# A gated mix of attention and a GEGLU layer: the order of head chains, last rows and one eviction around a nested product

## The chip, the cores and the metric

The kernel runs on one core of one Trainium2 chip. Its time is the device time of one execution in microseconds. The median of three runs of the kernel before is 1605.64 us (1605.62 to 1605.66). Engines are named as in the profile: PE is the matrix engine, DVE the vector engine, ACT the scalar engine, POOL the engine also called GpSimd, SP the one that issues the DMAs.

## The reference

Two branches over the same x (2048 tokens of 576 numbers) are mixed by a gate for each token:

```python
g = sigmoid((x * gate_w).sum(-1, keepdims=True))
a = attention(x, wq, wk, wv, wo, beta)        # 32 heads of 18, four segments of 512 tokens with a memory
b = (gelu(x @ w_gate) * (x @ w_up)) @ w_down  # 4608 hidden columns
return g * a + (1 - g) * b
```

For this change it matters that the second branch is three large products over 4608 hidden columns, and that the softmax of 128 pieces (a head, a segment) is worked in between them.

## The kernel before

**Steps.** The hidden columns are cut into 36 groups of 128, f, and the tokens into two halves, p. Each pair (f, p) is one call of `step(v)` (line 1428 on), v = 2f + p, 72 in all. Four steps make a block, fb = v // 4, and i4 = v % 4 is the place in it. A step computes gate and up of 128 hidden columns for 1024 tokens, by a scheme of Strassen's kind: sums of blocks of the weights are multiplied with sums of blocks of x, in three PSUM banks named V, G (in the code X) and U (in the code Y), and copies and adds on DVE carry one result into the next. Every operand is a pair of f16 parts, high and low, so each product is three matmuls for each block of rows: high by high, high by low, low by high. `product` (line 527) issues six matmuls of 512 columns, `rest` (1299) and `low_rests` (1304) the last 64 rows of the 576.

**The nested product.** In blocks from fb = 1 on, the product in V of the block's first group (i4 = 0 and 1) is itself split by the same scheme into seven products of 256 columns. Six of them are computed ahead, in the step before the one that needs them, in four pieces, `nest(at, 0)` to `nest(at, 3)` (line 1380): steps with i4 = 3 compute them for the next block's i4 = 0, steps with i4 = 0 for i4 = 1. I call these two the carrying steps, and the steps that use the result (i4 = 0 and 1) the nested steps. Piece 2, which the text calls the third, is six matmuls, the last three into the half A of bank V, which DVE then adds to a held tile (line 1401). Piece 3, the fourth, is three matmuls into A again, and so waits for that add; DVE adds it too (1404). The seventh, `nest_last` (1406), stands in the nested step, behind X's first product.

**The down chains.** The third product, with w_down, runs one block late: `chains` (1266) calls `down` (1248) for 32 chains of a block, eight in each step. A chain is six matmuls of 288 columns into a bank dn (of two), and one DVE instruction (1264) that adds it to the result. `early` are the step's first five, `late` the last three. It reads w_down's pairs (`paird`, low part by POOL, line 402) and the hidden values' pairs (`hh`, tiles hhr and hhd, high part by ACT, 1286, low part by POOL, 1294).

**The softmax.** `scores(a)` (1160) issues four matmuls: two into st banks, one of 256 columns into dn, one of 128 into pv or, for odd a, the other dn. DVE masks each and takes its maximum (1174). `powers` (1179) makes the exponentials on ACT and their pairs on POOL, and issues two transposing DMAs on SP. `values` (1197) is 20 short matmuls from them into bank pv, `normalize` (1212) what DVE does with the result.

**The end of a step.** `hidden` (1276) evicts bank G or U on DVE, times the gelu, into the hidden values; `end_pair` (1415), at the start of the next step, does this for the step before, and in between takes the mask passes of the last scores, first the dn pieces. In carrying steps `end_first` (1411) evicts G within the step itself. `hidden_pair` (1283) makes the pairs; in steps with i4 = 3 it leaves one low part on a list, which `hidden_lows` (1291) empties.

**What sets the order.** All four compute engines run in the order written in the code, so a step's text is the order of four queues; between engines only data and buffers make one wait for another. Where a step's call is moved, all that it issues on PE and DVE moves with it.

Of the kernel before, what the change touches and what calls it, by code (L numbers as in the profile page):

```python
# [43 lines left out]
def kernel(ctx: ExitStack, tc: tile.TileContext, xs, wqk, wv, wo, wgu, wd, beta, out):  # L44
# [8 lines left out]
    def bank(tag, bufs=1, dt=F32):  # L53
        return ps.tile([P, 512 if dt == F32 else 1024], dt, name=tag, tag=tag, bufs=bufs)
# [249 lines left out]
    def scale_g(f, cols=slice(0, KT * P)):  # L304
        if f < NF:
            r = raw_g[f].rearrange("p (a b) -> p a b", a=2)[:, :, cols]
            dve.tensor_scalar(r, r, scl[f // 2][0][:, 0:1], None, OP.mult)
# [16 lines left out]
    def sums_g(f):  # L324
        if f >= NF:
            return
        r = raw_g[f]
        g0, g2, u0, u2 = (r[:, o : o + 2 * P] for o in (0, 2 * P, KW, KW + 2 * P))
        g4, u4 = r[:, 4 * P : KW], r[:, KW + 4 * P :]
        pool.tensor_tensor(g2, g0, g2, OP.add)  # L330
        if f < 2 or f % 2 == 0:
            pool.tensor_tensor(g0, u0, g0, OP.subtract)
        pool.tensor_tensor(u0, g2, u0, OP.subtract)
        pool.tensor_tensor(u2, u2, u0, OP.subtract)
        pool.tensor_tensor(g4, u4, g4, OP.subtract)
# [7 lines left out]
    def low_g(f, b):  # L343
        for p in parts_g(f, b):
            pool.tensor_tensor(spot(f, *p, 1), raw_g[f][:, p[0] : p[1]], spot(f, *p, 0), OP.subtract)  # L345
# [18 lines left out]
    def nest_odd(b):  # L364
        if b < NB:
            nest_w[b] = nest_tile()
            r = raw_g[2 * b + 1]
            pool.tensor_tensor(nest_part(b)[1], r[:, KW : KW + 2 * P], r[:, : 2 * P], OP.subtract)

    def nest_pairs(b, i, what):  # L370
        if b >= NB:
            return
        a, r = nest_part(b)
        src, o = ((a, W00), (r[:, P:], W11), (r, WS3), (a, WS2))[i]
        n = src.shape[1]
        hi, lo = (nest_w[b][:, (o + 7 * j) * P : (o + 7 * j) * P + n] for j in range(2))
        if "h" in what:
            act.activation(hi, src, AF.Copy)
        if "l" in what:
            pool.tensor_tensor(lo, src, hi, OP.subtract)  # L380
# [11 lines left out]
    def scale_d(f):  # L392
        r = raw_d[f]
        dve.tensor_scalar(r, r, scl[f // 2 + 1][0][:, 1:2], None, OP.mult)
# [5 lines left out]
    def low_d(f):  # L400
        t = pair_d[f]
        pool.tensor_tensor(t[:, 1], raw_d.pop(f), t[:, 0], OP.subtract)  # L402
# [702 lines left out]
    with tc.tile_pool(name="keep", bufs=2, side="right", reuse_waits="tile") as kp, ExitStack() as tail:  # L1105
# [91 lines left out]
        def values(a):  # L1197
            kk, e = divmod(a, 2)
            if e == 0:
                pvb[kk] = bank("pv")  # L1200
            o = pvb[kk]
            pr = turned_p.pop(a)
            v = vts[kk // 4]
            c0 = (kk % 4) * VC
            for qi in range(4):
                ov = o[:, (4 * e + qi) * VC : (4 * e + qi + 1) * VC]
                for kb in range(qi + 1):
                    for i in range(2):
                        pe.matmul(ov, pr[:, 10 * i + COL[qi] // P + kb], v[:, 4 * e + kb, c0 : c0 + VC],  # L1209
                                  start=kb == 0 and i == 0, stop=kb == qi and i == 1)  # L1210
# [80 lines left out]
        def hidden_lows():  # L1291
            while lows:
                hh, t = lows.pop()
                pool.tensor_tensor(hh[:, 1], t, hh[:, 0], OP.subtract)
# [23 lines left out]
        def weights_nest(fb, i4, at):  # L1318
            if i4 == 1 and at == 2 and fb:
                for f in (2 * fb, 2 * fb + 1):  # L1320
                    scale_d(f)
            if i4 == 2 and at == 1:
                if fb:
                    scale_g(2 * fb + 3, FRONT)
                    sums_g(2 * fb + 2)
                nest_odd(fb + 1)
            if i4 == 2 and at == "late":
                for i in range(2):
                    nest_pairs(fb + 1, i, "hl")
                nest_sums(fb + 1)  # L1330
            if i4 == 2 and at == 2:
                for i in (2,) if fb else (2, 3):
                    nest_pairs(fb + 1, i, "hl")
            if i4 == 3 and at == 0 and fb:
                nest_pairs(fb + 1, 3, "hl")
                hidden_lows()

        def weights_high(fb, i4):
            n0 = 2 * fb
# [4 lines left out]
        def weights_low(fb, i4):  # L1344
            n0 = 2 * fb
            low_g(n0 + 1 + i4 // 2, i4 % 2)
            if i4 == 3:
                for f in (n0, n0 + 1):
                    low_d(f)

        def weights_load(fb, i4):
            n0 = 2 * fb
            if i4 == 1:
                load_g(n0 + 4)
            if i4 == 0 and fb:
                load_d(n0)
                load_d(n0 + 1)
            if i4 == 3:
                load_g(n0 + 5)
# [20 lines left out]
        def nest(at, n):  # L1380

            if at is None:
                return
            b, p = at
            if n == 0:
                nested[at] = bank("V")
                holds[p] = kp.tile([P, L], F32, name=f"hold{p}", bufs=1)
            B, A = (nested[at][:, i * HX : (i + 1) * HX] for i in range(2))
            h0, h1 = (holds[p][:, i * HX : (i + 1) * HX] for i in range(2))
            if n == 0:  # L1390
                nest_product(b, B, W00, X00, p, True)
                nest_product(b, A, WS3, XT3, p)
                dve.tensor_copy(h1, A)
            if n == 1:
                nest_product(b, A, W11, XT4, p)
                dve.tensor_copy(h0, A)
                dve.tensor_copy(A, B)
            if n == 2:
                nest_product(b, B, W01, X10, p)
                nest_product(b, A, WS2, XT2, p)  # L1400
                dve.tensor_tensor(h0, A, h0, OP.add)  # L1401
            if n == 3:
                nest_product(b, A, WS1, XT1, p)
                dve.tensor_tensor(h1, A, h1, OP.add)
# [6 lines left out]
        def end_first():  # L1411
            hidden(*ends[0])
            ends[0] = ends[0] + (True,)
# [14 lines left out]
        def step(v):  # L1428

            f, p = divmod(v, 2)  # L1430
            fb, i4 = divmod(v, 4)
            c, e = 2 * p, 2 * p + 1
            k = v - LAG
            on = lambda i: 0 <= i < 2 * H
            early = range(8 * i4, 8 * i4 + 5)
            late = range(8 * i4 + 5, 8 * i4 + 8)
            some = lambda b, js: chains(b, js) if b >= 0 else None
# [13 lines left out]
            at = (fb + 1, 0) if i4 == 3 and fb + 1 < NB else (fb, 1) if i4 == 0 and fb else None  # L1451
            if not fb:
                V, g1 = ahead.pop(v) if v in ahead else first_product(v)
            elif i4 < 2:
                V, g1 = nested[fb, p], gl_tile()
                if v != 4:
                    some(fb - 1, early[:1])
            else:
                V, g1 = bank("V"), holds[p]
                product(V, f, A22, x2_, 0, 4, True)  # L1460
            X, Y = bank("G"), bank("U")
            product(X, f, A11, x1, 0, 4, True)
            one = (2 if fb and i4 < 2 else 1) + (v == 4)
            if v == 4:
                dve.tensor_copy(Y, X)
                nest((1, 0), 2)
                some(0, early[:2])
                nest((1, 0), 3)
                some(0, early[2:3])
                nest_last(fb, V, p)  # L1470
                dve.tensor_copy(g1, V)
                nest_pairs_x(1, 1)
                some(0, early[3:4])
            elif fb and i4 < 2:
                nest_last(fb, V, p)
                dve.tensor_copy(g1, V)
                dve.tensor_copy(Y, X)
                put(2 * k - 1, 3)
                if on(k - 2):
                    values(2 * k - 3)  # L1480
            else:
                put(2 * k - 1, 3)
                dve.tensor_copy(Y, X)
# [6 lines left out]
            if v == 1:  # L1490
                scale_result()
            if v != 4:
                some(fb - 1, early[1 if fb and i4 < 2 else 0 : one])
            put(2 * k - 1, 2)
            puts.pop(2 * k - 1, None)
            if on(k - 2) and not (fb and i4 < 2):
# [13 lines left out]
            if fb:  # L1510
                weights_high(fb, i4)
                weights_low(fb, i4)
            weights_load(fb, i4)
            if v == 2 * NF - 2:
                sums_a(0)
# [77 lines left out]
            some(fb - 1, late[1:])  # L1593
            if on(k - 1):
                values(2 * k - 2)
            if v != 3:
                nest(at, 2)
            if low is not None:
                result_low(low)
            if fb:  # L1600
                low_rests(f, (X, U4, x1), (Y, UG, x2_))
                ends.append((f, c, X, g0))
                if at:
                    end_first()
            if on(k):
                puts[2 * k + 1] = scores(2 * k + 1)
            if v != 3:
# [159 lines left out]
        with tc.manual_schedule(engines=ORDERED):  # L1767
# [17 lines left out]
            fb = NB - 1  # L1785
# [88 lines left out]
```

## Time and profile before

| | |
|---|---|
| median of three runs | 1605.64 us |
| profiled execution | 1604.89 us |
| its span | 1603.2 us |
| granted PE clock | 1.000 |
| PE, DVE, ACT, POOL busy | 1559.9, 1257.4, 1208.8, 1123.7 us |

The span goes from the first to the last instruction of the profiled execution. Lines of a timeline begin with the start and the length in us from the span's start; a line can stand for several equal instructions in a row (x6), and its length then goes from the first one's start to the last one's end. A matmul's end is modelled: 512 columns are shown with 0.38 us, but six in a row start 0.215 us apart. In brackets stands for how long the engine was idle before, and what released it.

### The profile page before, as it was taken

To read this page: it belongs to the slowest core of one execution; us is meant where nothing else is said; L and a number is where in the kernel's file an instruction comes from. 1 tells how busy PE (TensorE), PEld (TensorE's weight loads), DVE (VectorE), ACT (ScalarE), POOL (GpSimd) and SP (SyncE) were. 2 spreads that over 40 slices of the span, in tenths; PEclk is the share of its full clock that TensorE was granted. 3 is DMA by queue.
4 is the path that set the end of the run, shared out by engine and by line. 5 is a ranking of instruction groups with operands and counts; after the bars stand their busy time and mean duration, and the time that the engine had idled before them with its cause. 6 is when DMAs were issued, how large, how long until landed. Compare 5 with 4: busy or idle time off the path is not lost.

```text
span 1603.2 us, 33958 instructions
## 1 busy us (share of the span) xinstructions
PE 1559.9 (97%) x12220; PEld 955.2 (60%) x12220; DVE 1257.4 (78%) x3254; ACT 1208.8 (75%) x2059; POOL 1123.7 (70%) x1220
## 2 busy tenths in 40 slices
PE   9999999999999999999999999999999999999999
PEld 5665655555555555556555555565555556556577
DVE  6788976778787888778787878787888778787565
ACT  7567544888888888888888888888888888787421
POOL 4345555877786868686776777776868686777597
PEclk9999999999999999999999999999999999999999
DMA  6534332576868687676777686879687777764546
GB/s 231 211 127 135 118 116 60 114 133 120 148 118 147 129 125 140 121 132 130 127 123 132 119 145 121 146 120 152 131 128 130 134 134 132 131 111 96 119 85 168
DMA packets 472833, 209.97 MB, mean 131 GB/s; under 512 B 427688, under 2 KB 437416, under 8 KB 472152
## 3 DMA queue, kind: packets, MB, share of 16 engines
q1 hardware_dynamic: 472664, 207.80, 65.7%
q8 instruction: 96, 1.57, 0.4%
q14 instruction: 73, 0.60, 0.1%
HBM read 91.87 MB, written 27.26 MB: 74 GB/s over the span
## 4 chain that ended last, share of the span: by engine, by line
PE 62%; POOL 12%; DVE 3%; ACT 3%; issue 1%; POOLq 0%; ACTq 0%; DVEq 0%
PE dn L1256 20%; PE U L532 14%; PE G L532 9%; PE V L532 5%; PE pv L1209 3%; PE V L1377 3%; POOL paird L402 2%; POOL pairg L345 2%; POOL pb L1192 2%; PE U L1302 1%; PE V L1307 1%; DVE gl L1279 1%; POOL x L1707 1%; PE V L1302 1%; POOL pairg L1690 1%
## 5 line engine op out<-in xcount | busy, mean ns | idle before, releaser
L1192 POOL TENSOR_TENSOR pb<-pb,ph 128x896 f16<-128x896 f32 (+1 forms) x256 | 368.4, 1439 | 273.2 <-ACT ph L1191 263.2
L532 PEld LDWEIGHTS <-pairg 128*128 128x128 f16 x2592 | 250.6, 98 | 261.4 <-issue 12.4
L1256 PE MATMUL dn<-paird,hhr 128*128 128x288 f16 x2115 | 331.3, 286 | 24.3 <-DVE mx L1174 20.9
L1190 ACT ACTIVATE pb<-pb,mb,esc 128x512 f32<-128x512 f32 (+3 forms) x512 | 305.0, 643 | 5.5 <-issue 0.4
L1264 DVE SCALAR_TENSOR_TENSOR acc<-dn,ev,acc 128x288 f32<-128x288 f32 x533 | 265.2, 513 | 45.8 <-PE dn L1256 38.5
L1256 PEld LDWEIGHTS <-hhr 128*128 128x128 f16 x2160 | 205.5, 98 | 106.7 <-issue 41.5
L1256 PE MATMUL dn<-paird,hhd 128*128 128x288 f16 x1275 | 211.7, 286 | 10.7 <-DVE mx L1174 7.0
L532 PE MATMUL G<-x,pairg 128*128 128x512 f16 x864 | 209.9, 379 | 1.1 <-DVE gl L1279 1.0
L532 PE MATMUL U<-xt,pairg 128*128 128x512 f16 x864 | 209.9, 379 | 0.0
L1191 ACT ACTIVATE ph<-pb 128x896 f16<-128x896 f32 (+1 forms) x256 | 188.5, 736 | 8.1
L345 POOL TENSOR_TENSOR pairg<-raw,pairg 128x384 f16<-128x384 f32 (+2 forms) x144 | 157.8, 1117 | 17.7 <-ACT pairg L341 17.7
L1256 PEld LDWEIGHTS <-hhd 128*128 128x128 f16 x1296 | 123.7, 98 | 63.6 <-issue 20.5
L1174 DVE CUSTOM_DVE_ANT_0 pb<-st,mask 128x512 f32<-128x512 f32 (+1 forms) x256 | 157.0, 613 | 0.0
L1174 DVE CUSTOM_DVE_ANT_0 pb<-dn,mask 128x256 f32<-128x256 f32 (+1 forms) x192 | 67.0, 374 | 91.7 <-PE dn L1171 89.9
L1185 ACT ACTIVATE mb<-mx,esc 128x4 f32<-128x4 f32 x128 | 36.8, 288 | 103.3 <-DVE mx L1174 103.3
L1377 PE MATMUL V<-xt,nest 128*128 128x256 f16 x714 | 105.9, 272 | 0.3 <-DVE hold L1401 0.2
L532 PE MATMUL U<-x,pairg 128*128 128x512 f16 x432 | 105.0, 379 | 0.4 <-DVE gl L1554 0.3
L532 PE MATMUL V<-x,pairg 128*128 128x512 f16 x426 | 103.9, 380 | 0.2
L1297 ACT ACTIVATE gl<-gl,sc 128x512 f32<-128x512 f32 x110 | 75.7, 714 | 29.8 <-DVE gl L1554 18.2
L1209 PEld LDWEIGHTS <-pt 128*128 128x128 f16 x2560 | 83.4, 96 | 5.5
L1209 PE MATMUL pv<-vt,pt 128*128 128x37 f16 x2560 | 84.6, 179 | 0.0
L1297 ACT ACT_TABLE_LOAD x65 | 83.4, 1283 | 1.1
(369 smaller groups left out, 3100.5 us busy)
## 6 DMA issues: line engine op xcount, KB each, us to landing
raw<-in_wgu_dram SPq DMA_DIRECT2D x36, 640.0 KB
rawd<-in_wd_dram SPq DMA_DIRECT2D x36, 288.0 KB
qt<-qk SPq DMA_DIRECT2D x132, 72.0 KB
kt<-qk SPq DMA_DIRECT2D x132, 72.0 KB
qk<-stage SPq DMA_DIRECT2D x36, 256.0 KB
qt<-qk SPq DMA_DIRECT2D x132, 36.0 KB
kt<-qk SPq DMA_DIRECT2D x132, 36.0 KB
vp<-vstage SPq DMA_DIRECT2D x16, 296.0 KB
```

The lines of the kernel that those rows point to most:

```text
L345: pool.tensor_tensor(spot(f, *p, 1), raw_g[f][:, p[0] : p[1]], spot(f, *p, 0), OP.subtract)
L532: pe.matmul(o, w[:, i, (a + k) * P : (a + k + 1) * P], x[:, b + k], start=start and k == 0 and i == 0 and b == h, stop=k == 1 and i == 1, ...
L1174: dve.tensor_tensor_reduce(scored(a, qi), out[qi], mask[:, L - (qi + 1) * P :], 1.0, -3e38, OP.add, OP.max, mx[a][:, qi : qi + 1])
L1185: act.activation(b, mx.pop(a), AF.Copy, bias=LN256, scale=esc[:, 1, c : c + 1])
L1190: act.activation(r, r, AF.Exp, bias=b[:, qi : qi + 1], scale=esc[:, 0, c : c + 1])
L1191: act.activation(h[:, cols], p, AF.Copy)
L1192: pool.tensor_tensor(low[:, cols], p, h[:, cols], OP.subtract)
L1209: pe.matmul(ov, pr[:, 10 * i + COL[qi] // P + kb], v[:, 4 * e + kb, c0 : c0 + VC], start=kb == 0 and i == 0, stop=kb == qi and i == 1)
L1256: pe.matmul(o[:, :NH], hh[:, a, q * P : (q + 1) * P], w[:, b, n * NH : (n + 1) * NH], start=i == 0, stop=i == 5)
L1264: dve.scalar_tensor_tensor(av, o[:, :NH], ev, av, OP.mult, OP.add)
L1297: act.activation(t, o, AF.Gelu_apprx_tanh, scale=scl[f // 2][0][:, 2 + c : 3 + c])
L1377: pe.matmul(o, w[:, (7 * c + i) * P : (7 * c + i + 1) * P], x[d], start=start and n == 0, stop=n == 2, skip_group_check=True)
```

## The change

Four moves, none of which adds or drops an instruction of the computation:

- In nested steps (but v = 4) the first down chain goes from ahead of X's product to behind the last nested product and the copies of V and X, next to the second one.
- In the same steps the values of the score before last go from ahead of the second chain to behind it.
- In steps with i4 = 3, the low part of hh that was left on the list is made behind the low parts of the next weights on POOL, not ahead of them.
- In carrying steps (but v = 3) the last rows of G and U and G's eviction go ahead of the third nested piece.

```diff
@@ weights_nest
             if i4 == 3 and at == 0 and fb:
                 nest_pairs(fb + 1, 3, "hl")
-                hidden_lows()
@@ step
             elif i4 < 2:
                 V, g1 = nested[fb, p], gl_tile()
-                if v != 4:
-                    some(fb - 1, early[:1])
@@ step
                 dve.tensor_copy(g1, V)
                 dve.tensor_copy(Y, X)
                 put(2 * k - 1, 3)
-                if on(k - 2):
-                    values(2 * k - 3)
             else:
                 put(2 * k - 1, 3)
                 dve.tensor_copy(Y, X)
@@ step
             if v != 4:
-                some(fb - 1, early[1 if fb and i4 < 2 else 0 : one])
+                some(fb - 1, early[:one])
+                if fb and i4 < 2 and on(k - 2):
+                    values(2 * k - 3)
             put(2 * k - 1, 2)
@@ step
             if fb:
                 weights_high(fb, i4)
                 weights_low(fb, i4)
+                hidden_lows()
             weights_load(fb, i4)
@@ step
                 values(2 * k - 2)
-            if v != 3:
-                nest(at, 2)
             if low is not None:
                 result_low(low)
             if fb:
@@ step
                 ends.append((f, c, X, g0))
                 if at:
                     end_first()
+            if v != 3:
+                nest(at, 2)
             if on(k):
                 puts[2 * k + 1] = scores(2 * k + 1)
```

## The prediction

> **What bounds the kernel.** I read the busy line of the page first, then the waits of PE, then the timeline of one block, engine by engine.
>
> ```profile
> PE 1559.9 (97%) x12220; PEld 955.2 (60%) x12220; DVE 1257.4 (78%) x3254; ACT 1208.8 (75%) x2059; POOL 1123.7 (70%) x1220
> ```
>
> PE is busy for 1559.9 of 1603.2 us, so a change of order can win about what PE idles, 43 us by this count. PE's rows in the view of waits say where most of it lies (us in total, times, longest):
>
> ```profile
> PE dn L1256 <- DVE mx L1174: 27.8, 32, 0.9
> PE dn L1256 <- POOL paird L402: 6.9, 14, 0.5
> ...
> PE V L1377 <- DVE hold L1401: 0.2, 1, 0.2
> ```
>
> Two kinds of wait make 34.7 us, both at a down chain (line 1256), and both so even (27.8/32 = 0.87, 6.9/14 = 0.49) that one block can stand for all. Both lie at the first head chain of a nested step. Here is PE from the end of a step with i4 = 0 into the one with i4 = 1:
>
> ```profile
> 724.54 0.81 PE L1377 MATMUL V<-xt,nest 128*128 128x256 f16 x6
> 725.28 0.39 PE L1307 MATMUL G<-x,pairg 64*128 64x512 f16 x1
> ...
> 725.51 0.38 PE L1171 MATMUL st<-kt,qt 54*128 54x512 f16 x2
> ...
> 725.88 0.50 PE L1377 MATMUL V<-xt,nest 128*128 128x256 f16 x3
> 727.25 0.53 PE L1256 MATMUL dn<-paird,hhr 128*128 128x288 f16 x3 [0.87 <-DVE mx L1174]
> ...
> 727.98 1.46 PE L532 MATMUL G<-x,pairg 128*128 128x512 f16 x6
> 729.28 0.49 PE L1377 MATMUL V<-xt,nest 128*128 128x256 f16 x3
> 729.61 0.67 PE L1209 MATMUL pv<-vt,pt 128*128 128x37 f16 x20
> 730.12 0.53 PE L1256 MATMUL dn<-paird,hhr 128*128 128x288 f16 x3
> ```
>
> In order: the third nested piece, the last rows, the scores, the fourth piece, the first head chain after its wait, X's product, the last nested product, the values, the second head chain. From start to start X's product takes 1.30 us and the last nested product 0.33; the fourth piece, of the same shape, is thus issued by 725.88 + 0.33 = 726.21, and PE issues nothing until 727.25: 1.04 us (the view says 0.87, since it counts from the modelled end of the matmul before). What the chain waits for is on DVE:
>
> ```profile
> 724.12 0.93 DVE L1264 SCALAR_TENSOR_TENSOR acc<-dn,ev,acc 128x288 f32<-128x288 f32 x2
> 725.39 0.42 DVE L1401 TENSOR_TENSOR hold<-V,hold 128x256 f32<-128x256 f32 x1 [0.34 <-PE V L1377]
> 725.78 0.75 DVE L1279 SCALAR_TENSOR_TENSOR gl<-G,sc,gl 128x512 f32<-128x512 f32 x1
> 726.45 0.41 DVE L1404 TENSOR_TENSOR hold<-V,hold 128x256 f32<-128x256 f32 x1
> 726.78 0.41 DVE L1174 CUSTOM_DVE_ANT_0 pb<-dn,mask 128x256 f32<-128x256 f32 x1
> ...
> 727.12 0.28 DVE L1174 CUSTOM_DVE_ANT_0 pb<-dn,mask 128x128 f32<-128x128 f32 x1
> ```
>
> The scores hold both dn banks; DVE frees the first at about 727.2, after the add of the third piece, G's eviction and the add of the fourth. X's product writes G and needs only that eviction, over at 726.53. The step with i4 = 0 begins in the same way, with POOL as a second wait (rows of POOL, DVE, ACT and PE in order of time):
>
> ```profile
> 701.80 1.16 POOL L1294 TENSOR_TENSOR hhd<-gl,hhd 128x512 f16<-128x512 f32 x1
> ...
> 702.92 2.04 POOL L345 TENSOR_TENSOR pairg<-raw,pairg 128x384 f16<-128x384 f32 x2
> ...
> 703.22 0.93 DVE L1264 SCALAR_TENSOR_TENSOR acc<-dn,ev,acc 128x288 f32<-128x288 f32 x2
> ...
> 703.44 0.71 ACT L1297 ACTIVATE gl<-gl,sc 128x512 f32<-128x512 f32 x1
> ...
> 704.48 0.42 DVE L1401 TENSOR_TENSOR hold<-V,hold 128x256 f32<-128x256 f32 x1 [0.33 <-PE V L1377]
> ...
> 704.91 2.51 POOL L402 TENSOR_TENSOR paird<-rawd,paird 128x576 f16<-128x576 f32 x2
> ...
> 704.97 0.50 PE L1377 MATMUL V<-xt,nest 128*128 128x256 f16 x3
> ...
> 706.34 0.53 PE L1256 MATMUL dn<-paird,hhr 128*128 128x288 f16 x3 [0.87 <-DVE mx L1174]
> 706.71 0.28 PE L1256 MATMUL dn<-paird,hhd 128*128 128x288 f16 x1
> ...
> 707.48 0.41 PE L1256 MATMUL dn<-paird,hhd 128*128 128x288 f16 x2 [0.48 <-POOL paird L402]
> ...
> 707.72 1.46 PE L532 MATMUL G<-x,pairg 128*128 128x512 f16 x6
> ...
> 710.58 1.46 PE L532 MATMUL V<-x,pairg 128*128 128x512 f16 x6
> ```
>
> **The head chains move behind the nested product.** No matmul is added or dropped, so only idle time changes. X's product and the last nested product, 1.30 + 0.33 = 1.63 us, now stand between the fourth piece and the first chain. That is more than the 1.04 us for which the chain waited, so this idle time goes: 32 x 1.04 = 33.3 us. At i4 = 0 the chain's fifth matmul was due at 706.34 + 4 x 0.12 = 706.83 (three take 0.37) and came at 707.48: 0.65 us, 14 times, 9.1 us. POOL is done by 704.91 + 2.51 = 707.42. In the new order the fourth piece starts at 705.36 (below), X's product at 705.69, the chain at 707.32, its fifth matmul at 707.8. The wait goes, by 0.4 us. Together 42.4 us.
>
> **What is late next.** X's product wants G; the last nested product wants the add of the fourth piece, 1.30 us back; V's product wants V copied, and there the two chains and the values (0.73 + 0.73 + 0.51 us, by the starts above) stand as cover instead of one chain and the values. On DVE the first chain's eviction falls behind the two copies and the 512 wide mask pass; the next user of a dn bank comes behind V's and Y's products, so nobody waits. The values come later in the step, yet hardly later on the clock: at i4 = 1 at 726.56 (below) + 1.63 + 2 x 0.73 = 729.65 against 729.61, at i4 = 0 sooner; their readers on DVE stand behind the eviction of Y. Cost of these: nothing. If the cover went, each would cost what it is short, at most 0.5 us in 16 steps, 8 us.
>
> **The held low part on POOL.** In steps with i4 = 3, hh's low part (1.16 us) goes behind two pairg and two paird subtractions. POOL's sum is the same, and the order of these alone changes; paird is ready 1.1 us sooner, and hh's low part last, at 707.42. The first chain of the next step reads it in its sixth matmul, at about 707.9: 0.5 us of room. Elsewhere the list is empty and the moved call does nothing. ACT's queue is not touched; the result's low part, with its DMAs, falls in steps with i4 = 2, in which no piece is moved, so SP's queue is not crossed either.
>
> **Last rows and G's eviction ahead of the third piece.** PE does the same work in another order. On DVE the eviction (0.67 us from start to start: 725.78 to 726.45) now stands ahead of the add that the fourth piece waits for. The last rows start where the third piece did, 724.54, plus a gap of 0.1 (such as lies between the third piece's six matmuls, 6 x 0.11, and 725.28), and G is complete 0.39 later, at 725.03; DVE is free at 725.05. So the eviction starts at 725.07, the add at 725.74, not 725.39: 0.35 later. The fourth piece came 725.88 - 725.39 = 0.49 after the add's start, though the scores in between were short enough; it does so again, 0.35 later. This is a new idle gap. At i4 = 3 the eviction needs also the gelu that ACT ends at 703.44 + 0.71 = 704.15, as DVE gets free (703.22 + 0.93); eviction 704.20, add 704.87, fourth piece 705.36 instead of 704.97: 0.39. Sum: 16 x 0.35 + 16 x 0.39 = 11.8 us, plus about 0.6 us in the last step of this kind, where no scores stand in between (the eviction's 0.67 less the gap of 0.1; its fourth piece waits already):
>
> ```profile
> 1477.41 0.49 PE L1377 MATMUL V<-xt,nest 128*128 128x256 f16 x3 [0.19 <-DVE hold L1401]
> ```
>
> It pays for itself only in that X's product finds G free. Without it, X's product would start after the eviction, at 726.53 + 0.06; with it, at 725.88 + 0.35 + 0.33 = 726.56. This part alone is therefore worth nothing, by these rows, and the bounds of the gap are 0 (the add is not held up) and 0.75 us (the eviction comes a whole length later).
>
> **The sum.** 42.4 - 11.8 - 0.6 = 30.0 us. From the profiled execution's 1604.89 us this makes 1574.9; the three timed runs lie 0.75 higher at their median, 1605.64, so the forecast is 1575.6 us.
>
> **A rule that bears on it.** The change brings DVE's scaling of the next weights forward against POOL:
>
> ```profile
> 712.13 1.15 POOL L1294 TENSOR_TENSOR hhr<-hold,hhr 128x512 f16<-128x512 f32 x1
> ...
> 712.26 1.44 DVE L307 TENSOR_SCALAR raw<-raw,sc 128x768 f32<-128x768 f32 x1
> 713.65 0.69 DVE L1526 COPY gl<-U 128x512 f32<-128x512 f32 x1
> ...
> 715.63 1.46 PE L532 MATMUL U<-xt,pairg 128*128 128x512 f16 x6
> ```
>
> The scaling ended when POOL's subtraction did, plus 0.42. The subtraction hangs on ACT and stays at 712.13, while DVE and PE come 1.3 us sooner at i4 = 0. If the scaling is held until 713.28 all the same, U's copy stays at 713.7 and ends at 714.35; the product at 715.63, moved to 714.33, would wait 0.1 us, 15 times: 1577.1 us. The Trainium skill, SBUF — State Buffer, section Who interferes with whom, says that such a pass of VectorE and a GpSimd instruction exclude each other for a whole instruction, whichever came second; the row agrees with it.
>
> **The rivals.**
> 1. Forecast: both waits go, the gap of 0.35 to 0.39 comes. 1575.6 us, chance 0.64.
> 2. No new gap, the fourth piece is not held up. 1605.64 - 42.4 = 1563.2 us. Against it: DVE works in order, and the last case above shows PE waiting for that add. 0.10.
> 3. POOL stays on the path at i4 = 0: it ends 0.5 us or more later than in the trace, and the chain waits for hh's low part as it did for paird. The 9.1 us stay: 1584.7 us. For it: POOL runs without a gap from 701.80. 0.16.
> 4. The scaling held by POOL: 1577.1 us, 0.04.
> 5. Slower. DVE is made to wait for ACT's gelu at i4 = 3 with the add, the masks and so the scores' banks behind it. From 30.0/16 = 1.9 us of delay the gain is gone; at 2.5 us it is 1605.64 - 30.0 + 40 = 1615.6 us. For it: ACT ends its gelu at the very moment that DVE wants it. Against it: nothing moved is ahead of it on ACT. 0.03.
> 6. The waits only move, because another engine sets the length of a block: 1605.6 us, 0.03. Against it, over one block and a bit:
>
> ```profile
> 642.00:727.00 85.00, 82.16 (x692) 50.33 (x692) 68.45 (x186) 70.00 (x116) 58.93 (x62) 1.00 0.70 125
> ```
>
> ACT, the next one, is busy 70.00 of 85.00 us.
>
> **The numbers.** The likeliest case gives 1575.6. The range goes from rival 2, 1563, to a gap of 0.75 us in all 32 steps, 1575.6 + 32 x 0.38 = 1588, which takes in rival 3. A measurement of this kernel tells about 0.2%, 3.2 us, from no change: faster 0.64 + 0.10 + 0.16 + 0.04 = 0.94, same 0.03, slower 0.03.
>
> **What would show it.** In the changed profile the two rows at line 1256 are gone from PE's waits; the row V <- hold of line 1401 stands there some 33 times, at 0.1 to 0.3 us (by the modelled ends); X's product follows the fourth piece without a gap; PE's busy time is the same. Rows for paird, hhd or hhr in PE's waits would speak for rival 3, rows DVE L1279 <- ACT gl of some us for rival 5, a first chain that still waits for mx against the whole.

## The result and the profile after

| | before | after |
|---|---|---|
| median of four runs | 1605.63 us | 1576.42 us |
| lowest to highest | 1604.57 to 1605.66 | 1576.22 to 1576.78 |
| profiled execution, its span | 1604.89, 1603.2 us | 1576.45, 1574.7 us |
| ratio, 95% interval | | 0.982, 0.9803 to 0.9837 |

The changed kernel is 29.2 us faster; the forecast was 30.0 us (1575.6 us). The busy line of its page, and PE's rows in the view of waits (the lines of code behind the moves have shifted by one or two: 1377 is now 1376, 1401 is 1400):

```profile
PE 1561.6 (99%) x12220; PEld 960.3 (61%) x12220; DVE 1248.7 (79%) x3254; ACT 1208.7 (77%) x2059; POOL 1128.9 (72%) x1220
```

```profile
PE G L813 <- POOL onesb L808: 1.0, 1, 1.0
PE G L532 <- DVE gl L1279: 1.0, 2, 0.6
PE V L1376 <- DVE hold L1400: 1.0, 2, 0.5
...
PE dn L1256 <- DVE acc L1264: 0.2, 1, 0.2
```

PE does the same work (1561.6 us against 1559.9) in a span that is 28.5 us shorter. Both rows that made 34.7 us are gone: no chain waits for mx or for paird. The row of the third piece's add, 0.2 us before, is 1.0 us now, but from two steps only. In 31 more steps the fourth piece also comes 0.4 us later, and this view doesn't show it, because its wait lies within the modelled tail of the scores. One has to read it from the starts. PE, from the late values to the next product in V, in the step with i4 = 0 and into that with i4 = 1:

```profile
713.65 0.67 PE L1209 MATMUL pv<-vt,pt 128*128 128x37 f16 x20
714.26 0.39 PE L1307 MATMUL G<-x,pairg 64*128 64x512 f16 x1
...
714.58 0.83 PE L1376 MATMUL V<-xt,nest 128*128 128x256 f16 x6
715.34 0.39 PE L1171 MATMUL st<-kt,qt 54*128 54x512 f16 x2
...
715.92 0.49 PE L1376 MATMUL V<-xt,nest 128*128 128x256 f16 x3
716.25 1.46 PE L532 MATMUL G<-x,pairg 128*128 128x512 f16 x6
717.54 0.49 PE L1376 MATMUL V<-xt,nest 128*128 128x256 f16 x3
717.87 0.53 PE L1256 MATMUL dn<-paird,hhr 128*128 128x288 f16 x3
...
719.86 1.46 PE L532 MATMUL V<-x,pairg 128*128 128x512 f16 x6
```

X's product follows the fourth piece at once (715.92 + 0.33), and the chain follows the nested product. The same two ends in the trace of before, for i4 = 1 and (first line) the start for i4 = 0:

```profile
703.12 0.66 PE L1209 MATMUL pv<-vt,pt 128*128 128x37 f16 x20
...
724.02 0.67 PE L1209 MATMUL pv<-vt,pt 128*128 128x37 f16 x20
...
730.85 1.46 PE L532 MATMUL V<-x,pairg 128*128 128x512 f16 x6
```

From values to V's product it was 730.85 - 724.02 = 6.83 us and is 719.86 - 713.65 = 6.21: 0.62 us won at i4 = 1. At i4 = 0 it was 710.58 - 703.12 = 7.46 us. After:

```profile
694.04 0.66 PE L1209 MATMUL pv<-vt,pt 128*128 128x37 f16 x20
...
696.29 0.49 PE L1376 MATMUL V<-xt,nest 128*128 128x256 f16 x3
696.62 1.46 PE L532 MATMUL G<-x,pairg 128*128 128x512 f16 x6
...
698.24 0.53 PE L1256 MATMUL dn<-paird,hhr 128*128 128x288 f16 x3
...
700.22 1.46 PE L532 MATMUL V<-x,pairg 128*128 128x512 f16 x6
```

700.22 - 694.04 = 6.18 us, 1.28 us won. With 18 steps of the one kind (16 with i4 = 1, and the two with i4 = 0 that had no wait for paird) and 14 of the other this makes 18 x 0.62 + 14 x 1.28 = 29.1 us, near the measured 29.2. The count is a round one: in the last nested step the first chain had not waited, and V's product, 1481.34 - 1475.57 = 5.77 us behind the values before, comes 1452.78 - 1446.58 = 6.20 behind them now, 0.43 lost; two of the 18 won 0.83 and 0.88, which makes up for it.

### The profile page after: what moved, and what is told of

Same layout as the page of the kernel before. It is cut to its first block, busy times and chain, and to the rows that moved or that the text cites. A ratio compares the mean times of both kernels' runs of the same rounds, so it can differ in the third digit from the quotient of the medians.

```text
span 1574.7 us, 33958 instructions
## 1 busy us (share of the span) xinstructions
PE 1561.6 (99%) x12220; PEld 960.3 (61%) x12220; DVE 1248.7 (79%) x3254; ACT 1208.7 (77%) x2059; POOL 1128.9 (72%) x1220
## 5 line engine op out<-in xcount | busy, mean ns | idle before, releaser
L1297 ACT ACTIVATE gl<-gl,sc 128x512 f32<-128x512 f32 x110 | 75.7, 715 | 34.5 <-DVE gl L1552 22.9
L1376 PEld LDWEIGHTS <-nest 128*128 128x128 f16 x714 | 66.8, 97 | 43.4 <-issue 17.0
L1294 POOL TENSOR_TENSOR hhr<-gl,hhr 128x512 f16<-128x512 f32 x64 | 78.1, 1226 | 11.6 <-ACT hhr L1286 11.6
```

What stands on the lines that cost most here:

```text
L1297: act.activation(t, o, AF.Gelu_apprx_tanh, scale=scl[f // 2][0][:, 2 + c : 3 + c])
L1376: pe.matmul(o, w[:, (7 * c + i) * P : (7 * c + i + 1) * P], x[d], start=start and n == 0, stop=n == 2, skip_group_check=True)
```

## The experiments

Theory 1 is the prediction's account of the gain: cover ahead of the chains is all of it, and the moved last rows with G's eviction give nothing. Theory A is its account of the new gap ahead of the fourth piece: DVE does the eviction ahead of the third piece's add. Its rival, theory B: PE's own order makes the gap, since the last rows no longer stand between the third piece and the fourth. All ratios below are to the kernel before, run on the same chip. It took 1605.14 us in the measurement of the first four runs and 1605.22 in that of the last four, against 1605.63 beside the changed kernel, so a difference between one of these runs and the changed kernel is uncertain by some 0.5 us.

**Chains alone.** The kernel before, with the first chain moved:

```diff
-                if v != 4:
-                    some(fb - 1, early[:1])
...
-                some(fb - 1, early[1 if fb and i4 < 2 else 0 : one])
+                some(fb - 1, early[:one])
```

> The kernel before with only the first head chain moved behind the last nested product; values, POOL's order, last rows and G's eviction stay as before. Theory 1 (the chains' cover is the whole gain, and the last rows with G's eviction ahead are worth nothing, since X's product starts 2.57 us after the values either way): 1574 to 1578 us, and no row dn <- mx among PE's waits. Rival (the earlier eviction of G is what lets X's product start): X's product inherits 0.3 to 0.7 us of the chain's wait in 32 steps, 1586 to 1600 us, with a row G <- DVE gl of line 1279 among PE's waits.

Measured: 1576.74 us, ratio 0.9823 (0.9809 to 0.9838). One move alone is worth the whole change. No chain waits for mx or paird; X's product waits for G instead, 7.6 us in 35 cases by the modelled ends:

```profile
PE G L532 <- DVE gl L1279: 7.6, 35, 0.6
...
PE pv L1209 <- DMA pt<-pb: 1.0, 1, 1.0
```

**Last rows and eviction alone.** The kernel before, with only the third nested piece put behind the last rows and `end_first`:

```diff
-            if v != 3:
-                nest(at, 2)
             if low is not None:
...
                 if at:
                     end_first()
+            if v != 3:
+                nest(at, 2)
```

> The kernel before with only the last rows and G's eviction ahead of the third nested piece; the head chain stays ahead of X's product. Theory 1: the fourth piece comes 0.4 us later, so the masks behind it free the chain's bank 0.38 us later; at i4 = 0 the wait for POOL takes that up (its end is fixed), so 18 of the 32 steps pay: 1612 us. Rival (the earlier eviction helps by itself): 1605.6 us or less. A plain count of 32 steps would give 1618 us.

Measured: 1612.81 us, ratio 1.0046 (1.003 to 1.0063), 7.7 us slower than before (1605.14 in this job). With the chain still first, the later fourth piece delays the masks that free its bank. PE of this run, first the way into a step with i4 = 0, then into one with i4 = 1:

```profile
705.63 0.66 PE L1209 MATMUL pv<-vt,pt 128*128 128x37 f16 x20
...
713.07 1.46 PE L532 MATMUL V<-x,pairg 128*128 128x512 f16 x6
...
726.51 0.67 PE L1209 MATMUL pv<-vt,pt 128*128 128x37 f16 x20
...
730.12 0.53 PE L1256 MATMUL dn<-paird,hhr 128*128 128x288 f16 x3 [0.86 <-DVE mx L1174]
...
733.73 1.46 PE L532 MATMUL V<-x,pairg 128*128 128x512 f16 x6
```

At i4 = 1 values to V's product take 7.22 us, 0.39 more than before; at i4 = 0 7.44 against 7.46, nothing more, since there the chain had to wait for POOL anyway and the later start only took that wait up. 18 x 0.39 = 7.0 us.

**Last rows and eviction put back.** The changed kernel with the lines of the last diff the other way round.

> The changed kernel with the last rows and G's eviction put back behind the third nested piece; chains, values and POOL's order stay changed. Theory 1 (this part is worth nothing): 1575 to 1578 us. Rival (it is needed to free G): 1586 to 1600 us.

Measured: 1574.78 us, ratio 0.981 (0.9795 to 0.9825): 1.6 us less than the changed kernel (1.2 if each is taken from its own kernel before), by 0.1%, near what a measurement tells, though the runs do not overlap (1574.34 to 1575.02 against 1576.22 to 1576.78). So this part gives nothing with the chains moved and costs 7.7 us without them. Here X's product waits for G instead:

```profile
712.53 0.67 PE L1209 MATMUL pv<-vt,pt 128*128 128x37 f16 x20
...
714.39 0.50 PE L1376 MATMUL V<-xt,nest 128*128 128x256 f16 x3
715.09 1.46 PE L532 MATMUL G<-x,pairg 128*128 128x512 f16 x6 [0.20 <-DVE gl L1279]
```

The values of that step began at 712.53, so X's product comes 2.56 us behind them, against 716.25 - 713.65 = 2.60 in the changed kernel, and 32 x 0.04 = 1.3 us is the size of the difference. X's product starts 715.09 - 714.39 = 0.70 us behind the fourth piece, not 0.33: the early eviction exchanges a wait of 0.37 us for G for a delay of 0.41 ahead of the fourth piece.

**Eviction behind the add.** The changed kernel, with PE's order as changed and DVE's as before:

```diff
             if fb:
                 low_rests(f, (X, U4, x1), (Y, UG, x2_))
                 ends.append((f, c, X, g0))
-                if at:
-                    end_first()
             if v != 3:
                 nest(at, 2)
+            if fb and at:
+                end_first()
```

> The changed kernel, but on DVE the eviction of G stands behind the add of the third piece again; PE's order stays changed (last rows ahead of the third piece). Theory A, as in the prediction (the new gap before the fourth piece comes from DVE's order): the fourth piece starts about 1.9 us after the values instead of 2.27, X's product at the same time as in the changed kernel, 1576 us. Theory B (the gap comes from PE's order: the last rows no longer stand between the third and the fourth piece, so the add can't start sooner): the fourth piece stays at 2.27 us, and the eviction now holds up X's product by 0.3 us in 32 steps, 1586 us.

Measured: 1586.59 us, ratio 0.9884 (0.9869 to 0.9898). Rows of PE and DVE of this run:

```profile
716.54 0.67 PE L1209 MATMUL pv<-vt,pt 128*128 128x37 f16 x20
...
718.33 0.42 DVE L1400 TENSOR_TENSOR hold<-V,hold 128x256 f32<-128x256 f32 x1 [0.76 <-PE V L1376]
...
718.81 0.49 PE L1376 MATMUL V<-xt,nest 128*128 128x256 f16 x3
...
719.47 1.45 PE L532 MATMUL G<-x,pairg 128*128 128x512 f16 x6 [0.17 <-DVE gl L1279]
```

DVE stands idle for 0.76 us until the third piece is done, and the add starts 718.33 - 716.54 = 1.79 us behind the values. In the changed kernel, with the eviction ahead of it, it starts 715.45 - 713.65 = 1.80 us behind them (rows of DVE):

```profile
714.75 0.75 DVE L1279 SCALAR_TENSOR_TENSOR gl<-G,sc,gl 128x512 f32<-128x512 f32 x1
715.45 0.42 DVE L1400 TENSOR_TENSOR hold<-V,hold 128x256 f32<-128x256 f32 x1
```

The fourth piece stays at 2.27 us, and X's product comes 719.47 - 716.54 = 2.93 us behind the values instead of 2.60, held up by the eviction: 32 x 0.33 = 10.6 us, near the 10.2 measured. Theory A falls, theory B holds: the third piece itself comes later, 714.58 - 713.65 = 0.93 us behind the values in the changed kernel instead of 724.54 - 724.02 = 0.52, because the last rows stand ahead of it, and the fourth follows the third by the same 1.34 us in the kernel before (725.88 - 724.54) and in the changed one (715.92 - 714.58).

Not all of this is a wait for the add. From the scores to the fourth piece it is 715.92 - 715.34 = 0.58 us in the changed kernel and was 725.88 - 725.51 = 0.37 before, so 0.21 us are a wait. (0.37 is what the scores take without one: from scores to a chain that waits for nothing it is 268.49 - 268.12 in the changed kernel. In the kernel before PE's own work filled the 1.34 us.) The other 0.20 lie ahead of the scores, which start 715.34 - 713.65 = 1.69 us behind the values, not 725.51 - 724.02 = 1.49, with the same matmuls ahead of them: PE has two more gaps of 0.1 us there (last section).

**The order on POOL put back.** The changed kernel with `hidden_lows()` behind `nest_pairs` again, as before.

> The changed kernel with hh's low part back in its old place on POOL, ahead of the pairg and paird subtractions. Theory 1 (the room at the chain covers either order): POOL ends at the same time with paird as the last job, 0.4 us before the chain's fifth matmul needs it; 1576.4 us, within 1 us, no row dn <- paird among PE's waits. Rival (the order on POOL is what took the 6.9 us of paird waits away): up to 9 us more, 1585 us.

Measured: 1576.75 us, ratio 0.9823 (0.9808 to 0.9837), 0.3 us from the changed kernel. In this run paird ends at 695.48 + 2.52 = 698.00, and the chain starts at 697.86, with its fifth matmul due 0.49 later:

```profile
695.48 2.52 POOL L402 TENSOR_TENSOR paird<-rawd,paird 128x576 f16<-128x576 f32 x2
...
697.86 0.53 PE L1256 MATMUL dn<-paird,hhr 128*128 128x288 f16 x3
```

That the chain came later took the wait away, not the order on POOL.

**Values put back.** The changed kernel with the values of nested steps ahead of the two chains.

> The changed kernel with the values of nested steps back ahead of the two head chains. Theory 1 (the same work between the copy of V and its next product, in another order, and the banks are free either way): 1576.4 us, within 1 us. Rival (values there wait for their transposed tiles, or give the chains the cover that they need): 0.2 us or more in some of the 32 steps, 3 to 8 us to the one side or the other.

Measured: 1577.61 us (1576.57 to 1578.2), ratio 0.9826 (0.981 to 0.9843), 1.2 us above the changed kernel and within what can be told. Its waits have one row that the changed kernel lacks, pv <- DMA pt<-pb with 1.0 us, once, the same as in the run with the chains alone; both have the values early.

**Values between the third and the fourth piece.** The changed kernel, with the eviction behind the add as above, and in carrying steps:

```diff
-            if on(k - 1):
+            if on(k - 1) and not at:
                 values(2 * k - 2)
...
             if v != 3:
                 nest(at, 2)
             if fb and at:
                 end_first()
+            if on(k - 1) and at:
+                values(2 * k - 2)
```

> The changed kernel, with the values of carrying steps between the third and the fourth nested piece (they stood ahead of the last rows), and G's eviction behind the third piece's add on DVE. Theory B (the gap is missing cover on PE between the two pieces): the 0.51 us of values fill it; X's product starts about 2.44 us after the late chains instead of 2.60, then limited by G's eviction; 32 x 0.16 = 5 us less, 1571 us. Theory A (DVE's order makes the gap): no better than the run with the eviction behind the add, 1586 us.

Measured: 1570.44 us (1570.35 to 1572.73), ratio 0.9787 (0.9773 to 0.9802), 6.0 us less than the changed kernel and the best of all. PE and DVE:

```profile
691.84 0.39 PE L1307 MATMUL G<-x,pairg 64*128 64x512 f16 x1
...
692.83 0.66 PE L1209 MATMUL pv<-vt,pt 128*128 128x37 f16 x20
...
693.37 0.74 DVE L1279 SCALAR_TENSOR_TENSOR gl<-G,sc,gl 128x512 f32<-128x512 f32 x1
...
693.80 0.50 PE L1376 MATMUL V<-xt,nest 128*128 128x256 f16 x3
694.17 1.46 PE L532 MATMUL G<-x,pairg 128*128 128x512 f16 x6
```

The 0.51 us of values now cover the add. X's product starts when G's eviction ends (693.37 + 0.74 = 694.11), as expected of theory B. With a gap of 0.1 us ahead of the last rows, the late chains end at 691.74, and X's product comes 2.43 us behind them, not 2.60: 32 x 0.17 = 5.4 us. The values there with the eviction left ahead of the add were not run, so how much of this the order on DVE gives is not shown.

**Chains between X's product and the nested one.** The changed kernel with the two chains one place further ahead:

```diff
             elif fb and i4 < 2:
+                some(fb - 1, early[:one])
                 nest_last(fb, V, p)
...
-                some(fb - 1, early[:one])
+                some(fb - 1, () if fb and i4 < 2 else early[:one])
```

> The changed kernel with the two head chains between X's product and the last nested product instead of behind both. The cover ahead of the first chain falls from 1.63 to 1.30 us, which still is more than the 1.0 us that the banks need; but the copy of V then ends behind the chains, and V's next product has only the 0.51 us of values as cover. Theory (V's copy is the next wait, as in the prediction's list of what is late next): 0.5 us in 32 or 33 steps, 1592 us, a row V <- DVE gl of the copy among PE's waits. Rival (any place behind X's product does): 1576 us.

Measured: 1593.75 us, ratio 0.9929 (0.9914 to 0.9944), 17.3 us slower than the changed kernel. PE's waits and the place:

```profile
PE V L532 <- DVE gl L1474: 13.0, 33, 0.9
```

```profile
725.46 0.67 PE L1209 MATMUL pv<-vt,pt 128*128 128x37 f16 x20
726.50 1.46 PE L532 MATMUL V<-x,pairg 128*128 128x512 f16 x6 [0.37 <-DVE gl L1474]
```

The chain's own bank is free in time, but V's product starts 1.04 us behind the values rather than 0.51: 33 x 0.53 = 17.5 us. It waits for the copy of V, as the prediction's list of what is late next had it, with a price of 0.5 us in each step; it had counted 16 steps, and both kinds pay, 33.

## Why the prediction was right, and where not

- **The waits that go.** Right, and the whole of the gain: the run with the chains alone gives it. At i4 = 0 the room for the fifth matmul was put at 0.4 us and that for hh's low part at 0.5 us. With the order on POOL put back, paird is ready 0.35 us ahead of the fifth matmul. In the changed kernel POOL's last job ends at 698.35 (next fence), and the chain's sixth matmul is due at 698.24 + 5 x 0.12 = 698.85: 0.5 us.

```profile
694.71 2.52 POOL L402 TENSOR_TENSOR paird<-rawd,paird 128x576 f16<-128x576 f32 x2
697.18 1.17 POOL L1294 TENSOR_TENSOR hhd<-gl,hhd 128x512 f16<-128x512 f32 x1
```

- **The new gap.** The size came out right, in part by luck: 0.35 and 0.39 were forecast, and the fourth piece starts 2.27 and 2.25 us behind the values where it was 725.88 - 724.02 = 1.86 and 704.97 - 703.12 = 1.85, so 0.41 and 0.40. The step "the eviction starts at 725.07, the add at 725.74" failed as a cause. Two delays had nearly the same length, DVE's (the eviction) and PE's (the third piece 0.41 us later behind the last rows). I had worked out when G is complete and when DVE is free, but not when the third piece ends in its new place. With DVE's order undone the gap stayed. The forecast also took all of it for a wait for the add; it laid the 0.49 us from the add's start to the fourth piece of before to the add, though the scores' own time ended there too. The wait is 0.21 us; the other 0.20 are two more gaps on PE between matmuls with 128 and with 64 or 54 rows, for which the sum had no term. So a wait put too long and a cost put at nothing made up for each other.
- **This part worth nothing.** Right to 1.6 us with the chains moved. The forecast had not said that by itself it costs 7.7 us.
- **The sum.** 29.2 us measured, 30.0 forecast; the two gaps 0.06 and 0.01 us larger make 16 x 0.07 = 1.1 us of difference, and the last step cost 0.43 us, not 0.6.
- **What would show it.** The row of the add was forecast some 33 times at 0.1 to 0.3 us; it stands there twice. The gap exists, but the view counts from modelled ends, and the scores' tail hides it. That row could not test it.
- **The rivals.** No gap (1563.2 us): no. POOL on the path: no; the changed kernel has no wait for paird, hhd or hhr among PE's, nor has the run with POOL's order put back. DVE held up by ACT's gelu: no; the row DVE gl L1279 <- ACT gl L1297 stands among DVE's waits with 2.0 us in two cases, and stood there with 2.1 in two before. The waits only move: no, since the time fell. The scaling held by POOL: the scaling of 768 elements took 871 ns in the mean of 17, not 1378 (the row of before has 23.4 us in 17), so it was held up less when it came sooner:

```profile
L307 DVE TENSOR_SCALAR raw<-raw,sc 128x768 f32<-128x768 f32 x17 | 14.8, 871 | 0.0
```

In the block of the lines above it was POOL's subtraction that took long instead, 1.48 us against 1.16 for the next:

```profile
701.58 0.81 DVE L307 TENSOR_SCALAR raw<-raw,sc 128x768 f32<-128x768 f32 x1
...
701.92 1.48 POOL L1294 TENSOR_TENSOR hhd<-gl,hhd 128x512 f16<-128x512 f32 x1
703.36 1.16 POOL L1294 TENSOR_TENSOR hhr<-hold,hhr 128x512 f16<-128x512 f32 x1
```
The Trainium skill, SBUF — State Buffer, section Who interferes with whom, has it that the one that comes first holds the shared ports for a whole instruction; this pair of rows agrees as to who pays, though the subtraction is 0.32 us longer than the next one, less than the 0.47 for which it overlaps the scaling (701.58 + 0.81 - 701.92). The price moved to POOL, where nothing on PE waited for it.

## What to carry to other kernels

If an engine that is the bound waits at a place always for the same length, look for work in its own queue that doesn't need what it waits for, and put as much of it ahead as the wait is long; here 1.63 us of products stood ready behind a wait of 1.04. Then ask of each moved piece what it was covering: the last rows had covered an add, and moved away they opened a wait of 0.21 us that 0.51 us of other work could fill. When two queues both change at a point, work out the new time of both before naming the cause, and test by undoing the order of one queue alone. Read the delay from start to start, since a wait can hide behind a modelled end.

## What the runs showed of the hardware

A change on PE from matmuls with 128 rows to matmuls with 64 or 54 rows comes with a gap of about 0.1 us, and so does the way back. In the changed kernel's step above the gaps lie between the values' end (713.65 + 0.51) and the last rows at 714.26, between the last rows (0.23 by the starts 725.28 and 725.51 of before) and the third piece at 714.58, and between that (6 x 0.11) and the scores at 715.34. By the starts in the trace of before it is so wherever last rows follow a matmul of 128 rows and 512 columns: 0.31 us from the one to the other in 68 places, not 0.22. Where last rows and scores stand next to each other, as before the change, no gap lies between them, so keeping them together saves two such changes.

The weight loads of PE, in rows named PEld, show what is different there (kernel before):

```profile
704.37 0.10 PEld L1307 LDWEIGHTS <-pairg 64*128 64x128 f16 x2 [0.21 <-issue]
704.38 0.39 PE L1307 MATMUL G<-x,pairg 64*128 64x512 f16 x1
...
704.39 0.32 PEld L1171 LDWEIGHTS <-qt 54*128 54x128 f16 x4
...
704.60 0.38 PE L1171 MATMUL st<-kt,qt 54*128 54x512 f16 x2
...
707.60 1.08 PEld L532 LDWEIGHTS <-pairg 128*128 128x128 f16 x6
```

The scores' first load starts 0.21 us ahead of their first matmul, and that of X's product 0.12 ahead (its matmul starts at 707.72); the last rows' load starts only with their matmuls. A load takes 0.10 us, as long as the gap. That the load which isn't done ahead makes the gap is likely by this, but no run here tests it.
